# Attention through packed queries and a squared-ReLU layer on one core: the noughts' products between the first steps, 29 behind pv in place of 105 from the start

## The chip, the cores and the metric

The kernel runs on one core of a Trainium2 chip. The metric is device time in microseconds (us) from the launch to the end of the one program on that core; several runs are taken and their median is given. A core has a matrix engine (PE, with a weight loader written PEld in the profile), a vector engine (DVE), a scalar engine (ACT), a general engine (POOL), a queue engine (SP) that here only issues DMAs, and 16 DMA engines. Each engine works through its own list of instructions in order; where one needs another's result, it waits on a semaphore.

## What is computed

There are 8 batches of 8 heads, 576 rows per head and 64 columns, and 32 packed rows p per head. The reference is, cut to its core:

```python
def sm_attn(qq, kk, vv):
    s = scale * np.matmul(qq, kk.transpose(0, 1, 3, 2))
    s = s - np.max(s, axis=-1, keepdims=True)
    a = np.exp(s)
    a = a / (np.sum(a, axis=-1, keepdims=True) + 1e-09)
    return np.matmul(a, vv)
p_packed = sm_attn(p, k, v)              # 32 rows per head
out = sm_attn(q, p_packed, p_packed)     # 576 rows per head
x = out.transpose(0, 2, 1, 3).reshape(8 * 576, 8 * 64)
r = np.maximum(x @ w_in, 0.0)            # 4608 x 2048
result = (r * r) @ w_out                 # 4608 x 512, float32
```

The products on PE take bfloat16 operands and add up in float32.

## The kernel before, in words

Everything is written out by hand in one long string of words, `ORDER` (lines 50 to 142). `run` (line 778) takes it word by word, and each word puts the instructions of one small step at the end of the lists of the engines that it uses. So the string is the order on every engine, and nothing is rearranged later. A batch has two quads of four heads; the last two digits of a word such as `s100` are the batch and the quad. The words of batch 0, in the order in which they matter here:

- `pf`, `Lk`, `Lv`, `LA`, `LB`, `Wi`, `Wo` issue loads: the packed rows by SP, the keys, values, queries and weights by POOL. `P0` and `P1` scale the packed rows of two batches and turn them on DVE.
- `kT` turns the keys of one quad (DVE, line 361). `s1` multiplies them with the packed rows (PE, line 385: 24 products of 32 by 32 tiles per quad). `m1` takes the row maximum (DVE, line 411), `x1` the exponentials (ACT, line 423). `eT` turns them on PE (line 443), `eo` copies the turned block out of PSUM (DVE, line 431), and `rd` takes reciprocals of the sums.
- `pv` is the product with the values for both quads (PE, line 467). `pp` divides by the sums (DVE, line 480), `pt` turns that on PE (line 506) and `po` copies it out (ACT), and `bd` turns it in 32 by 32 blocks on DVE (line 488).
- `qA` and `qB` turn the first 256 and the last 320 queries (DVE, line 373). `zA` and `zB` multiply them with the packed result (PE, line 385 too). For each part then come the steps of the second softmax: `t` turn (DVE, line 528), `m` maximum (DVE, line 533), `s` difference (DVE, line 539, or POOL), `x` exponentials (ACT, line 545), `u` sums and reciprocals (DVE, lines 551 and 553), `a` product with these (POOL or DVE, line 559), `T` turn (DVE, line 573).
- `wa` and `wb` multiply the packed result into w_in (PE, line 584) and `Wa`, `Wb` copy it out. From there `h` is a block of the first layer (PE, line 600), `r` its ReLU, `q` the square into the tile gT, `o` a block of the second layer (PE, line 658), `c` a copy out of PSUM and `d` the store.

Batches overlap: while PE does `h` and `o` of one batch, the attention steps of the next stand between them. In batch 0 there is nothing to put between. There the string has words `Z` with a number, which call `busy` (line 341): so many products of a stretch of gT that holds noughts, as weights and as the moving operand, 288 columns wide, into a PSUM bank that nobody reads. No other engine waits for them, and they wait only once, for the memset of the noughts (line 197, DVE's first instruction). Being in PE's list like all else, the word that stands behind a `Z` starts no sooner than the `Z` has gone through. The order around them, lines 51 to 56 shortened to what stands on PE and what feeds it:

```python
Z32 s100 ... kT01 ... m100 Z4 s101 x100 m101 ... x101 Z13 eT00 eo00:v Z2 eT01 rd0 eo01:v
... Z4 pv0 pp0 qA01 Lk10 Z4 pt0 bd0 qA00 po0:a Z5 zA0 Lk11 tA00 tA01
mA01 mA00 sA01:v xA01 sA00:v uA01 xA00 qB00 Wo0 qB01 aA01:p uA00 Z33 zB0 wa00 Lv11
tB00 tB01 aA00:p Wa00:a mB00 Z5 wa01 mB01 sB00:p Wa01:a TA01 Z3 wb01 TA00 Lv10 wb00
```

The first `h` stands right behind these lines. The noughts' stretch of gT lies in a part that batch 3 fills much later.

Of the kernel before, what the change touches and what calls it, by code (L numbers as in the profile page):

```python
# [20 lines left out]
P = 128  # L21
# [3 lines left out]
S = T * NP  # L25
HALF = S // 2
# [24 lines left out]
pf Lk00 Lk01 Lv00 Lv01 I P0 LA0 P1 Wi00 kT00 Wi10 LB0 Z32 s100 Wi01  # L51
kT01 Wi11 m100 Z4 s101 x100 m101 Wi21 x101 Z13 eT00 eo00:v Z2 eT01 rd0 eo01:v
Wi20 Z4 pv0 pp0 qA01 Lk10 Z4 pt0 bd0 qA00 po0:a Z5 zA0 Lk11 tA00 tA01
mA01 mA00 sA01:v xA01 sA00:v uA01 xA00 qB00 Wo0 qB01 aA01:p uA00 Z33 zB0 wa00 Lv11
tB00 tB01 aA00:p Wa00:a mB00 Z5 wa01 mB01 sB00:p Wa01:a TA01 Z3 wb01 TA00 Lv10 wb00
xB00 sB01:v h0.0.8 h0.0.9 Wb01:a Wb00:v h0.0.1 h0.0.0 xB01 uB00 r0.0.8:a r0.0.1:a h0.0.2 uB01 r0.0.9:a aB00:p
r0.0.0:a h0.0.3 r0.0.2:v q0.0.4:a h0.0.11 Wo2 aB01:v h0.0.10 q0.0.0:a TB00 TB01 r0.0.3:a r0.0.10:v r0.0.11:a h0.1.0 h0.1.1
q0.0.1:v q0.0.5:a h0.1.9 r0.1.0:v h0.1.8 r0.1.1:a r0.1.9:v LA1 w100 w101 q0.1.0:v r0.1.8:a h0.1.10 W100:v W101:a h0.1.11
h0.1.3 q0.1.4:p h0.1.2 r0.1.10:a r0.1.3:v r0.1.11:a h0.0.4 kT10 r0.1.2:a LB1 h0.0.13 r0.0.4:a h0.0.5 q0.1.1:a h0.1.14 r0.0.13:v
q0.1.5:p h0.0.14 r0.0.5:v h0.1.13 r0.1.14:a kT11 h0.0.15 r0.0.14:a h0.0.6 q0.0.2:a h0.0.12 Wo1 r0.0.15:v s11 r0.1.13:a r0.0.12:v  # L60
r0.0.6:a Wo3 h0.1.15 q0.0.7:v q0.0.6:a h0.0.7 r0.1.15:v h0.1.4 r0.0.7:a Lv20 h0.1.6 m110 r0.1.4:a h0.1.5 r0.1.6:a h0.1.7
m111 h0.1.12 q0.0.3:a o2.0 x110 r0.1.5:v o2.1 r0.1.12:v q0.1.7:p o0.0 x111 o3.0 r0.1.7:a eT10 q0.1.6:a o0.1
Pr q0.1.2:v eT11 q0.1.3:v eo10:a o1.0 rd1 eo11:v o3.1 pv1 o1.1 pp1 o0.2 pt1 o1.2 bd1
po1:a o3.2 qA11 w011 w111 qA10 W011:a o0.3 W111:v o2.2 Lv21 o1.3 qB10 zA1 qB11 w010
o2.3 tA11 W010:a tA10 o3.3 mA11 zB1 mA10 sA11 w110 o0.4 sA10 tB11 W110:a o2.4 tB10
o1.4 mB11 xA11 o0.5 xA10 mB10 o1.5 uA10 o2.5 Lk20 sB11 o0.6 uA11 o0.7 xB11 aA10
o1.6 c0:a aA11 o1.7 sB10 o3.4 TA10 c1:a d0 TA11 o2.6 uB11 xB10 h1.0.1 Lk21 h1.0.6
Px o2.7 r1.0.1:v d1 r1.0.6:v o3.5 aB11 h1.0.0 c2:a h1.0.2 Pt o3.6 r1.0.0:a TB11 o3.7 r1.0.2:a
d2 Lk31 Pu:v q1.0.0:a h1.0.4 h1.0.3 c3:a o4.0 r1.0.3:v r1.0.4:a o5.0 kT20 q1.0.1:a h1.0.7 d3 h1.0.5
uB10 o5.1 r1.0.5:a o4.1 r1.0.7:v q1.0.2:a aB10 h1.0.10 h1.0.8 q1.0.3:v r1.0.10:a o4.2 kT21 Lq2 h1.0.9 r1.0.8:a  # L70
o5.2 r1.0.9:a h1.0.12 TB10 s12 q1.0.4:v r1.0.12:a h1.0.14 m120 o5.3 Lv30 r1.0.14:a h1.1.1 m121 h1.1.3 r1.1.1:a
o5.4 x120 r1.1.3:v h1.0.11 o4.3 r1.0.11:v x121 h1.1.7 kT31 h1.0.15 eT20 Lq3 q1.0.5:a o4.4 r1.0.15:v eT21
r1.1.7:v q1.0.7:a o5.5 rd2 eo20:v eo21:a h1.0.13 h1.1.2 r1.0.13:v o4.5 r1.1.2:v q1.0.6:a h1.1.6 pv2 r1.1.6:v h1.1.8
pp2 h1.1.0 q1.1.1:a r1.1.8:v Lk30 o5.6 qT21 q1.1.3:a o4.6 h1.1.12 r1.1.0:a bd2 pt2 qT20 o4.7 bs2:a
Lk40 h1.1.5 po2:v r1.1.12:a o5.7 q1.1.0:v c4:a h1.1.10 r1.1.5:v c5:a s22 d4 r1.1.10:v h1.1.4 o6.0 t221
r1.1.4:a h1.1.9 d5 o7.0 q1.1.2:a t220 h1.1.13 r1.1.9:a o6.1 qT30 r1.1.13:a Lq4 h1.1.11 q1.1.4:a m221 w120
w121 r1.1.11:a o6.2 m220 W121:a h1.1.14 h1.1.15 W120:v Lv31 o6.3 r1.1.14:a q1.1.6:a o7.1 o6.4 sb21:v r1.1.15:a
Lv40 o7.2 q1.1.5:a kT30 o7.3 q1.1.7:a o7.4 sb20:v Lk41 x221 o6.5 qT31 o7.5 x220 o6.6 su21
o6.7 o7.6 su20 c6:a o7.7 w020 a221 c7:a d6 w021 o8.0 W020:a a220 o8.1 d7 o8.2
aT21 W021:a o8.3 aT20 o8.4 Lq5 h2.0.1 h2.0.0 r2.0.1:v o8.5 r2.0.0:a o8.6 q2.0.0 h2.0.2 h2.0.3 r2.0.2:v  # L80
o9.0 Lk50 o8.7 r2.0.3:v h2.0.5 c8:a s13 q2.0.1 r2.0.5:a h2.0.4 d8 m130 o10.0 r2.0.4:a h2.0.6 kT40
h2.0.7 r2.0.6:a o10.1 r2.0.7:a q2.0.2 h2.0.10 Lk51 x130 m131 o9.1 h2.0.8 r2.0.10:a q2.0.3 o9.2 r2.0.8:a kT41
h2.0.13 x131 eT30 h2.0.9 r2.0.13:v o10.2 eo30:a rd3 r2.0.9:v h2.1.1 eT31 q2.0.4 h2.0.14 r2.1.1:a o10.3 r2.0.14:v
eo31:a h2.0.11 Lk61 o9.3 r2.0.11:v o9.4 h2.0.12 h2.1.5 q2.0.5 r2.0.12:a pv3 r2.1.5:v h2.0.15 q2.0.6 h2.1.4 pp3
r2.0.15:a o9.5 r2.1.4:v h2.1.6 bd3 pt3 q2.0.7 h2.1.0 bs3:a o9.6 r2.1.6:v r2.1.0:v Lv41 po3:a o9.7 q2.1.2
h2.1.8 q2.1.0 c9:a h2.1.2 r2.1.8:v s23 r2.1.2:a Lv50 d9 o11.0 t230 h2.1.3 h2.1.7 t231 o10.4 r2.1.3:a
w130 m230 r2.1.7:a w030 W130:a h2.1.10 q2.1.1 h2.1.9 q2.1.3 o10.5 W030:a m231 o10.6 o11.1 sb30:v r2.1.10:a
o11.2 r2.1.9:a sb31:v o10.7 x230 o11.3 q2.1.4 c10:a h2.1.15 qT40 o11.4 x231 h2.1.11 su30 r2.1.15:a w031
d10 r2.1.11:a w131 W031:a h2.1.14 su31 h2.1.13 o12.0 r2.1.14:a a230 o12.1 r2.1.13:a o12.2 W131:a q2.1.5 o12.3
a231 h2.1.12 o11.5 aT30 r2.1.12:a o12.4 aT31 o12.5 q2.1.6 q2.1.7 h3.0.5 h3.0.2 qT41 r3.0.5:a o12.6 h3.0.0  # L90
r3.0.2:v Lq6 o11.6 r3.0.0:a o12.7 h3.0.1 h3.1.1 r3.0.1:v c12:a o11.7 r3.1.1:v s14 d12 c11:a q3.0.0 h3.0.4
kT50 h3.0.3 r3.0.4:a o13.0 r3.0.3:a m140 d11 h3.0.9 Lk60 o14.0 r3.0.9:a q3.0.1 h3.1.3 x140 kT51 h3.1.0
o14.1 r3.1.3:a m141 o13.1 Lk70 r3.1.0:a h3.0.8 q3.0.2 eT40 x141 h3.0.7 r3.0.8:v o13.2 eo40:v r3.0.7:a h3.0.6
q3.1.0 o14.2 q3.0.4 r3.0.6:a eT41 rd4 q3.0.3 h3.0.11 eo41:a h3.1.2 r3.0.11:v o14.3 r3.1.2:v o13.3 h3.0.12 h3.0.10
q3.1.1 pv4 r3.0.10:a r3.0.12:v o14.4 Lv51 pp4 h3.0.13 q3.0.5 h3.0.14 r3.0.13:a bd4 o13.4 r3.0.14:v bs4:a pt4
Lv60 q3.0.6 h3.0.15 h3.1.8 o13.5 po4:v r3.1.8:a o14.5 r3.0.15:v s24 q3.0.7 h3.1.11 t240 h3.1.6 r3.1.11:a o13.6
t241 r3.1.6:a o13.7 w040 qT51 c13:a w041 h3.1.4 W040:a m241 o16.0 d13 h3.1.5 m240 r3.1.4:a o16.1
r3.1.5:a o14.6 W041:a sb41:v h3.1.9 h3.1.7 q3.1.2 o14.7 r3.1.7:a sb40:v r3.1.9:a w140 w141 x241 q3.1.3 h3.1.10
c14:v o16.2 W141:a h3.1.13 q3.1.4 d14 o15.0 su41 r3.1.10:a o16.3 x240 o15.1 r3.1.13:v W140:a h3.1.12 q3.1.5
o16.4 a241 o15.2 r3.1.12:a h3.1.14 su40 h3.1.15 o16.5 r3.1.14:a q3.1.6 o15.3 r3.1.15:a a240 o15.4 o16.6 q3.1.7  # L100
o15.5 aT40 aT41 o16.7 qT50 o15.6 c16:a h4.0.1 h4.0.4 Lq7 r4.0.1:v o15.7 d16 r4.0.4:v o17.0 c15:a
h4.0.3 h4.0.2 r4.0.3:v o17.1 r4.0.2:a d15 s15 q4.0.1 h4.0.0 kT60 h4.0.9 o17.2 r4.0.0:a m151 o17.3 r4.0.9:a
h4.0.6 m150 o17.4 r4.0.6:a h4.1.3 q4.0.0 x151 o17.5 kT61 o18.0 x150 o17.6 r4.1.3:v Lk71 h4.0.5 h4.0.13
rd5 r4.0.5:a o18.1 r4.0.13:v eT50 h4.0.11 eo50:v h4.0.12 eT51 q4.0.2 o17.7 r4.0.12:v r4.0.11:a o18.2 eo51:a c17:v
h4.1.2 h4.0.10 q4.0.6 r4.1.2:a pv5 d17 r4.0.10:a h4.0.7 Lv61 q4.1.1 h4.0.15 r4.0.7:a o19.0 q4.0.5 r4.0.15:a pp5
o19.1 q4.0.3 o19.2 Lv71 bd5 h4.0.8 pt5 bs5:v h4.1.11 r4.0.8:a o18.3 po5:v q4.0.4 h4.1.1 s25 r4.1.11:a
r4.1.1:v o18.4 qT60 h4.1.0 o18.5 t251 h4.1.6 o19.3 r4.1.0:a t250 r4.1.6:a o18.6 q4.1.0 h4.0.14 h4.1.10 m251
r4.0.14:a w050 r4.1.10:a w150 q4.0.7 W050:a h4.1.4 m250 h4.1.7 o18.7 r4.1.4:v W150:a o19.4 r4.1.7:v o19.5 q4.1.5
c18:a o19.6 q4.1.3 sb50:v o19.7 d18 h4.1.8 qT61 c19:a o20.0 x250 h4.1.5 sb51:v o21.0 d19 r4.1.5:a
o20.1 r4.1.8:a su50 o21.1 x251 h4.1.12 q4.1.2 h4.1.9 r4.1.12:a w151 a250 r4.1.9:a w051 h4.1.15 W151:a su51  # L110
o20.2 o21.2 r4.1.15:a q4.1.4 o21.3 W051:a a251 o20.3 h4.1.14 aT50 h4.1.13 aT51 s16 r4.1.14:a r4.1.13:v o20.4
kT70 h5.0.6 h5.0.8 r5.0.6:a m160 o20.5 r5.0.8:a h5.0.0 q4.1.7 o21.4 x160 m161 h5.0.4 o21.5 r5.0.0:a q4.1.6
eT60 r5.0.4:a kT71 h5.0.9 h5.0.1 x161 o20.6 r5.0.9:v o20.7 eo60:v r5.0.1:a h5.0.5 rd6 q5.0.4 c20:a eT61
r5.0.5:v h5.0.7 o21.6 q5.0.0 eo61:a q5.0.2 h5.0.10 d20 o22.0 r5.0.7:v r5.0.10:a o21.7 q5.0.3 h5.0.3 h5.0.2 c21:v
r5.0.3:a pv6 r5.0.2:a h5.1.0 d21 pp6 Lv70 h5.0.11 q5.0.1 r5.1.0:a o23.0 bd6 pt6 r5.0.11:v h5.0.13 bs6:a
# [29 lines left out]
class Kernel:  # L145
# [195 lines left out]
    def busy(self, n):  # L341

        ps = self.banks("idle").tile([P, 512], F32, name="ps_idle")
        for _ in range(n):
            self.nc.tensor.matmul(ps[:, :HALF], lhsT=self.nought[:, :P], rhs=self.nought, start=True, stop=True)  # L345
# [402 lines left out]
    def step(self, word):  # L748
        word, _, e = word.partition(":")
        engine = self.engines.get(e, self.nc.vector)  # L750
        q4 = self.NFB // 4
# [81 lines left out]
```

## Time and profile before

| what | value |
|---|---|
| three runs | 243.76, 243.35, 243.53 us; median 243.53 us |
| span of the profiled execution | 241.6 us (first to last instruction of the program) |
| PE busy | 235.7 us, 98% of the span, 2461 products |
| DVE, ACT, POOL busy | 203.3 us (84%), 142.0 us (59%), 74.7 us (31%) |
| products of noughts | 105, from 1.1 to 20.8 us |

The profile gives the profiled execution its span alone, and no other time of its own. The median of the runs is 1.9 us above that span; these 1.9 us lie before the program's first instruction and behind its last. Every position below is counted from the span's start. A product of PE is shown from its issue to its modelled end, so products that follow each other overlap in the rows; the distance from start to start is what each costs in a stream. In the views, "idle before <-X" is the time in which the engine had nothing to do just before that instruction and what ended it.

### The profile page before, as it was taken

To read this page: it belongs to the slowest core of one execution; us is meant where nothing else is said; L and a number is where in the kernel's file an instruction comes from. 1 tells how busy PE (TensorE), PEld (TensorE's weight loads), DVE (VectorE), ACT (ScalarE), POOL (GpSimd) and SP (SyncE) were. 2 spreads that over 40 slices of the span, in tenths; PEclk is the share of its full clock that TensorE was granted. 3 is DMA by queue.
4 is the path that set the end of the run, shared out by engine and by line. 5 is a ranking of instruction groups with operands and counts; after the bars stand their busy time and mean duration, and the time that the engine had idled before them with its cause. 6 is when DMAs were issued, how large, how long until landed. Compare 5 with 4: busy or idle time off the path is not lost.

```text
span 241.6 us, 6190 instructions
## 1 busy us (share of the span) xinstructions
PE 235.7 (98%) x2461; PEld 130.8 (54%) x2461; DVE 203.3 (84%) x459; ACT 142.0 (59%) x308; POOL 74.7 (31%) x123
## 2 busy tenths in 40 slices
PE   8999899999999999999999999999999999999994
PEld 5775564456544565456554654465545645565543
DVE  2679986999998789989998889997899879987650
ACT  2216993697898567956693647774495346733300
POOL 8636784594586163044403340002000000000000
PEclk9999999999999999999999999999999999999999
DMA  6999999999999979249932984317113211211224
GB/s 104 192 200 210 203 207 206 173 180 219 200 189 188 252 104 127 60 60 220 104 90 29 204 114 53 71 26 113 27 26 81 49 43 43 46 43 43 46 63 110
DMA packets 33404, 28.51 MB, mean 118 GB/s; under 512 B 8160, under 2 KB 28384, under 8 KB 33376
## 3 DMA queue, kind: packets, MB, share of 16 engines
q0 software_dynamic: 26848, 18.55, 54.4%
q1 hardware_dynamic: 6384, 9.51, 14.9%
q8 instruction: 19, 0.31, 0.5%
q14 instruction: 9, 0.07, 0.1%
q10 hardware_dynamic: 144, 0.07, 0.1%
HBM read 37.22 MB, written 9.44 MB: 193 GB/s over the span
## 4 chain that ended last, share of the span: by engine, by line
PE 94%; ACT 2%; DMA 2%; DVE 1%; SPq 0%; issue 0%; ACTq 0%; DVEq 0%
PE ps_o L658 52%; PE ps_h L600 26%; PE ps_idle L345 4%; PE ps_wp L584 4%; PE ps_s L385 3%; PE ps_e1T L443 2%; DMA gT<-in_p_dram 2%; PE ps_pv L467 1%; ACT r L605 1%; ACT gT L643 0%; PE ps_ppT L506 0%; ACT wp L429 0%; PE ps_o L663 0%; DVE kT L361 0%; SPq L278 0%; ACT e L545 0%
## 5 line engine op out<-in xcount | busy, mean ns | idle before, releaser
L658 PE MATMUL ps_o<-w_out_bf,gT 128*128 128x512 bf16 (+1 forms) x576 | 147.3, 378 | 0.0
L600 PE MATMUL ps_h<-a2T,wp 128*128 128x288 bf16 (+2 forms) x512 | 89.9, 286 | 1.3 <-DVE rs L553 0.6
L605 ACT ACTIVATE r<-ps_h 128x288 bf16<-128x288 f32 (+2 forms) x159 | 61.0, 415 | 47.2 <-PE ps_h L600 43.9
L658 PEld LDWEIGHTS <-gT 128*128 128x128 bf16 x576 | 54.4, 98 | 43.1 <-issue 3.2
L600 PEld LDWEIGHTS <-wp 128*128 128x128 bf16 x512 | 47.7, 98 | 42.4 <-issue 8.0
L607 DVE TENSOR_SCALAR r<-ps_h 128x288 bf16<-128x288 f32 (+2 forms) x97 | 41.8, 446 | 11.2 <-PE ps_h L600 10.6
L645 DVE TENSOR_TENSOR gT<-r 128x576 bf16<-128x576 bf16 (+2 forms) x104 | 45.1, 445 | 2.8 <-ACT r L605 1.8
L429 ACT CAST wp<-ps_wp 128x1024 bf16<-128x1024 f32 (+1 forms) x29 | 27.7, 974 | 9.1 <-PE ps_wp L584 9.0
L429 ACT COPY o_sb<-ps_o 128x512 f32<-128x512 f32 x26 | 15.2, 589 | 12.3 <-PE ps_o L658 11.9
L278 POOL DMA_DIRECT2D k_b<-in_k_dram x28 | 15.2, 544 | 16.2 <-DVE kT L361 7.6
L278 POOL DMA_DIRECT2D q_b<-in_q_dram x16 | 10.9, 684 | 29.9 <-DVE qT L373 25.4
L323 POOL DMA_DIRECT2D v_b<-in_v_dram x12 | 9.4, 781 | 31.5 <-PE ps_pv L467 30.5
L345 PE MATMUL ps_idle<-gT 128*128 128x288 bf16 x105 | 16.7, 314 | 1.1 <-DVE gT L197 1.1
L423 ACT ACTIVATE e<-ps_s,nm 128x576 bf16<-128x576 f32 x16 | 11.8, 742 | 7.6 <-DVE nm L411 7.6
L643 ACT ACTIVATE gT<-r 128x512 bf16<-128x512 bf16 (+1 forms) x21 | 14.0, 689 | 0.5 <-DVE r L607 0.3
L545 ACT ACTIVATE e<-d 128x576 f32<-128x576 f32 (+2 forms) x20 | 11.6, 599 | 4.2 <-DVE d L539 3.9
L345 PEld LDWEIGHTS <-gT 128*128 128x128 bf16 x105 | 10.6, 107 | 5.1 <-DVE gT L197 1.1
L411 DVE TENSOR_REDUCE nm<-ps_s 128x1 f32<-128x576 f32 x16 | 11.5, 740 | 1.2 <-PE ps_s L385 1.2
L373 DVE STREAM_TRANSPOSE qT<-q_b 128x576 uint32<-128x576 uint32 (+2 forms) x20 | 12.4, 631 | 0.0
L361 DVE STREAM_TRANSPOSE kT<-k_b 128x576 uint32<-128x576 uint32 x16 | 12.3, 767 | 0.1
L551 DVE TENSOR_REDUCE sums<-e 128x18 f32<-128x576 f32 (+2 forms) x20 | 12.2, 608 | 0.1
L533 DVE TENSOR_REDUCE mx<-s 128x18 f32<-128x576 f32 (+2 forms) x20 | 11.6, 609 | 0.0
(60 smaller groups left out, 185.3 us busy)
## 6 DMA issues: line engine op xcount, KB each, us to landing
out_dram<-o_sb SPq DMA_DIRECT2D x65, 128.0 KB, 3.0
v_b<-in_v_dram POOLq DMA_DIRECT2D x12, 256.0 KB, 6.4
w_out_bf<-in_moe_w_out_dram POOLq DMA_DIRECT2D x4, 512.0 KB, 12.2
q_b<-in_q_dram POOLq DMA_DIRECT2D x6, 288.0 KB, 5.6
q_b<-in_q_dram POOLq DMA_DIRECT2D x12, 144.0 KB, 6.3
k_b<-in_k_dram POOLq DMA_DIRECT2D x12, 108.0 KB, 3.6
gT<-in_v_dram POOLq DMA_DIRECT2D x4, 288.0 KB, 9.5
w_in_bf<-in_moe_w_in_dram POOLq DMA_DIRECT2D x4, 256.0 KB, 10.2
```

The lines of the kernel that those rows point to most:

```text
L278: engine.dma_start(x[n:], s[:P - n])
L345: self.nc.tensor.matmul(ps[:, :HALF], lhsT=self.nought[:, :P], rhs=self.nought, start=True, stop=True)
L361: self.nc.vector.transpose(t["kT"][:].rearrange("p s e -> p (s e)").bitcast(U32), t["k"][:].rearrange("p t d -> p (t d)").bitcast(U32))
L373: self.nc.vector.transpose(out.bitcast(U32), x.bitcast(U32))
L429: engine.copy(out, x)
L551: nc.vector.reduce_sum(out=sums[:, x], in_=t["e2"][:, x], axis=AX.X)
L600: self.nc.tensor.matmul(ps, lhsT=t["wp"][:, fb // n, fb % n * P:(fb % n + 1) * P], rhs=t["a2T"][:, s0:s1], start=(qd == 0), stop=(qd == se ...
L605: engine.activation(r, ps, ACT.Relu)
L607: engine.tensor_scalar_max(r, ps, 0.0)
L643: engine.activation(out, r, ACT.Square)
L645: engine.tensor_tensor(out=out, in0=r, in1=r, op=ALU.mult)
L658: self.nc.tensor.matmul(self.o[tt][:, e], lhsT=self.gT[:, fb, a:a + P], rhs=self.w_out_bf[:, fb, e], start=(i == 0), stop=(i == self.NFB - 1))
```

## The change

A word `Z` now carries two numbers, so many products of 512 columns and so many of 256, and the stretch of noughts grows from 288 to 512 columns, so that its memset does too. The five words ahead of `pv0` (`Z32`, `Z4`, `Z13`, `Z2`, `Z4`: 55 products) are gone. The five behind it stay at their places: `Z4` becomes `Z2.0`, `Z5` becomes `Z2.1` (twice), `Z33` becomes `Z18.1`, `Z3` becomes `Z1.1`. That is 25 products of 512 and 4 of 256 columns, 13,824 columns, the sum of 27 full ones, where 50 products of 288 had 14,400 columns; ahead of `pv0` 15,840 columns are gone. The string is broken into lines differently, so the lines of the program below it move up by ten. Every other word stands where it stood, and the lists of DVE, ACT, POOL and SP are the same.

```diff
-pf Lk00 Lk01 Lv00 Lv01 I P0 LA0 P1 Wi00 kT00 Wi10 LB0 Z32 s100 Wi01
-kT01 Wi11 m100 Z4 s101 x100 m101 Wi21 x101 Z13 eT00 eo00:v Z2 eT01 rd0 eo01:v
-Wi20 Z4 pv0 pp0 qA01 Lk10 Z4 pt0 bd0 qA00 po0:a Z5 zA0 Lk11 tA00 tA01
-mA01 mA00 sA01:v xA01 sA00:v uA01 xA00 qB00 Wo0 qB01 aA01:p uA00 Z33 zB0 wa00 Lv11
-tB00 tB01 aA00:p Wa00:a mB00 Z5 wa01 mB01 sB00:p Wa01:a TA01 Z3 wb01 TA00 Lv10 wb00
+pf Lk00 Lk01 Lv00 Lv01 I P0 LA0 P1 Wi00 kT00 Wi10 LB0 s100 Wi01 kT01 Wi11 m100 s101 x100 m101 Wi21 x101 eT00 eo00:v eT01
+rd0 eo01:v Wi20 pv0 pp0 qA01 Lk10 Z2.0 pt0 bd0 qA00 po0:a Z2.1 zA0 Lk11 tA00 tA01 mA01 mA00 sA01:v xA01 sA00:v uA01 xA00
+qB00 Wo0 qB01 aA01:p uA00 Z18.1 zB0 wa00 Lv11 tB00 tB01 aA00:p Wa00:a mB00 Z2.1 wa01 mB01 sB00:p Wa01:a TA01 Z1.1 wb01
...
-        self.nought = self.gT[:, 0, 3 * S:3 * S + HALF]
+        self.nought = self.gT[:, 0, 3 * S:3 * S + self.NE]
...
-    def busy(self, n):
+    def busy(self, n, short):
 
         ps = self.banks("idle").tile([P, 512], F32, name="ps_idle")
-        for _ in range(n):
-            self.nc.tensor.matmul(ps[:, :HALF], lhsT=self.nought[:, :P], rhs=self.nought, start=True, stop=True)
+        for m in [self.NE] * n + [self.NE // 2] * short:
+            self.nc.tensor.matmul(ps[:, :m], lhsT=self.nought[:, :P], rhs=self.nought[:, :m], start=True, stop=True)
...
-            self.busy(int(word[1:]))
+            self.busy(*map(int, word[1:].split(".")))
```

## The prediction

> **What bounds the kernel now.** I read the page's busy times first, then PE's timeline of the first 28 us, then busy times by stage, and last the noughts' own rows. The page says that PE is the bound, and that the noughts lie on the chain that ended last:
>
> ```profile
> PE 235.7 (98%) x2461; PEld 130.8 (54%) x2461; DVE 203.3 (84%) x459; ACT 142.0 (59%) x308; POOL 74.7 (31%) x123
> ...
> L345 PE MATMUL ps_idle<-gT 128*128 128x288 bf16 x105 | 16.7, 314 | 1.1 <-DVE gT L197 1.1
> ```
>
> The same by stage (window, its length, then each engine's busy time, the clock, the DMA share):
>
> ```profile
> 7.50:15.00 7.50, 7.48 (x160) 5.34 (x160) 4.68 (x11) 2.04 (x5) 3.52 (x6) 1.00 1.33 199
> 15.00:19.50 4.50, 4.50 (x57) 3.20 (x55) 4.03 (x13) 0.75 (x2) 2.65 (x5) 1.00 1.37 203
> 19.50:28.40 8.90, 7.62 (x89) 4.22 (x82) 8.74 (x23) 7.87 (x19) 5.52 (x8) 1.00 1.19 205
> 28.40:238.40 210.00, 209.93 (x2134) 113.90 (x2133) 183.22 (x406) 129.78 (x281) 56.62 (x92) 1.00 0.65 110
> ```
>
> From 28.4 us on PE is idle for 0.07 of 210 us: whatever time the steps before it lose or win, the end loses or wins. From 19.5 to 28.4 us DVE (third number) is busy for 8.74 of 8.90 us, so DVE sets that stretch, and the moment that counts is when it begins: DVE's first turn behind `zB0`, at 19.48 us. Before that PE looks full, but mostly with noughts; its timeline (start, length, and what it did):
>
> ```profile
> 1.08 6.21 PE L345 MATMUL ps_idle<-gT 128*128 128x288 bf16 x32 [1.08 <-DVE gT L197]
> 7.52 0.69 PE L385 MATMUL ps_s<-kT,pT 32*32 32x192 bf16 x24 [0.23 <-DVE kT L361]
> 8.15 0.66 PE L345 MATMUL ps_idle<-gT 128*128 128x288 bf16 x4
> 8.74 0.69 PE L385 MATMUL ps_s<-kT,pT 32*32 32x192 bf16 x24
> 9.36 1.77 PE L345 MATMUL ps_idle<-gT 128*128 128x288 bf16 x13
> ...
> 12.47 0.58 PE L467 MATMUL ps_pv<-gT,e1T 96*32 96x64 bf16 x48
> 12.98 0.66 PE L345 MATMUL ps_idle<-gT 128*128 128x288 bf16 x4
> ...
> 14.43 0.42 PE L385 MATMUL ps_s<-qT,ppd 32*32 32x256 bf16 x16
> 14.78 4.22 PE L345 MATMUL ps_idle<-gT 128*128 128x288 bf16 x33
> 18.93 0.47 PE L385 MATMUL ps_s<-qT,ppd 32*32 32x320 bf16 x16
> ```
>
> 32 products took 6.21 us at the start, 33 took 4.22 us later. The noughts' rows up to 5 us and behind 5.7 us (shortest, median, longest of one in ns) say why:
>
> ```profile
> L345 PE MATMUL ps_idle<-gT x17: 423/447/448, 1.1 to 4.9; 128*128 128x288 bf16 x17
> L345 PE MATMUL ps_idle<-gT x13: 286/286/286, 5.5 to 7.0; 128*128 128x288 bf16 x13
> ```
>
> From start to start one costs (4.22 - 0.29) / 32 = 0.123 us late, and in the first four us, by the trace's starts, 0.240 us: PE begins at half speed. The switch comes at 5.44 us, 4.36 us after its first product. (The page's clock row reads 9 throughout; it shows no early half clock, the durations do.) So before `s100`, the first useful product, PE has been brought to full speed by products that delay nothing: `s100` waited 0.23 us for DVE.
>
> **What the change does, part by part.** What PE sends during its first 4 us of dense work runs at half speed. The change moves that stretch from idle time onto the steps of batch 0.
>
> *Removed, ahead of pv.* 55 products. `Z32` frees nothing, `s100` waits for `kT` at 7.47 us. The others delayed their successors: `s101` had its keys at 8.31 and began at 8.74 us; `eT01` could start at about 11.15, when `x101` was read out, and began at 11.55 us.
>
> *The price of half speed on useful steps.* The trace has no small product at half clock. From the noughts, a step grows by 447/286 = 1.56 if its last product's length rules and by 0.240/0.123 = 1.95 if its stream rules. These steps are short, so I take 1.65 and keep both ends (about 0.2 us at `zB0` apart). Through the chain, with the other engines' lengths and hand-overs (about 0.05 us) as they are:
>
> - `s101` begins at 8.48, when the slower `s100` has streamed (8.74 before), lasts 1.14 (0.69) to 9.62 (9.43).
> - `m101`, `x101` follow: `m101` at 9.67 (9.48), `x101` read out at 11.29 (11.11).
> - `eT01` from 11.35 (11.55), 0.82 long (0.50), to 12.17 (12.05); its copy `eo01` to 12.77 (12.64).
> - second half of `pv` ends at 13.33 (13.05), so `pp` starts at 13.40 (13.13) and ends at 13.83.
>
> Up to here 0.27 us late: what the noughts' absence gives nearly pays for the clock.
>
> *Changed, behind pv.* In columns every word is smaller than before (1,024 for 1,152; 1,280 for 1,440; 9,472 for 9,504), but they cost by time. A 512-wide product at full clock is in the second layer's rows: 20 of them in 4.32 us, 0.216 us each. At half clock I estimate 512/288 x 0.240 = 0.427 us.
>
> - `Z2.0` behind `pv`: 2 x 0.427 = 0.85 where four took 0.49; it ends at about 14.0, behind `pp`'s end: `pt0` at 14.0 (13.61).
> - `Z2.1`: 2.5 x 0.427 = 1.07 (0.61). `zA0` is ready at 14.65 but starts at 15.3 (14.43), ends at 15.95 (14.85). Late by 1.0 to 1.1 us; DVE's eleven instructions up to `qB01` follow, to 19.75 (18.73).
> - `Z18.1` starts at 15.7 (14.78) and lasts 18 x 0.216 + 0.109 = 4.0 us at full clock, and half of what is left of the half-clock time more. I count the dense work from `pv`'s first half at about 11.95: plus 4.36 us gives full clock at 16.3, so 0.6 us of `Z18.1` is slow and it ends at 15.7 + 4.0 + 0.3 = 20.0. `zB0` then starts at 20.0 (18.93), DVE behind it at 20.5 (19.48).
> - `Z2.1` and `Z1.1` behind that are at full clock and a little shorter (0.54 for 0.61, 0.32 for 0.37); the words behind them wait for buffers that DVE and ACT free: nothing gained.
>
> *Unchanged or nearly.* The wider memset (0.18 us now, at most 0.1 more) lies in DVE's idle 1.33 us before its first use of the packed rows. No DMA moves past another; POOL's issues that wait for DVE come later with it, and the weights have time (`o2.0` at 33.3 us). No wait is added: PE has nothing queued for the noughts but their memset, done long before.
>
> **Sum:** DVE's turn at 20.5 instead of 19.48, +1.0 us. Span 241.6 + 1.0 = 242.6; the runs' median lies 1.9 above the span, which the change leaves: 243.53 + 1.0 = **244.5 us**.
>
> The unknown is which work brings up the clock. Recomputing the chain for other moments of full clock: 11 us gives -0.4, 12 gives -0.2, 13.5 gives 0, 14.5 +0.2, 15 +0.5, 16.3 +1.0, 17.5 +1.6, 18.5 +2.1, 19.6 +2.6. (Behind 15.7 us each us later costs half a us: a slow product does half its work.)
>
> A rule bears on this. The Trainium skill, "TensorE: Matmul & The Clock Gate", Part 1, says that the array stays at half rate until one busy window of about 3.4 us has passed, and that the windows run freely, whenever the kernel starts. The trace's 4.36 us agree with it. Counted from `pv`'s second half at 12.8 us, full clock would come between 16.2 and 19.6 us by that page, and the sum would be +1.0 to +2.6 us. The same section calls the warming's cost under 1% of a usual span, which either end of that is near.
>
> **The rivals.**
>
> - *The small products bring up the clock.* `s100` to `eT01` keep PE busy for 3.7 us between 7.5 and 12.2 us, with one gap of 0.8 us. For it: the trace shows no threshold. Against: they are a few tiles of 32, 25% of the array, or turns, with gaps, while the noughts that raised it filled all of it without one. If full clock comes at 11 us, `eT01` and all behind it run at full speed, the removed noughts' delay is won back: `pp` 0.25 us earlier, `zA0` at 14.15, `Z18.1` ends at 18.5, -0.4 us: 243.1. It ends not slower if full clock comes before 13.5 us; up to 14.9 us it costs under 0.5.
> - *The clock comes up late.* Noughts behind `pv` stand between short steps; if only an unbroken stretch counts, it begins with `Z18.1` at 15.3 to 15.7 us, and full clock comes at 18.5 to 20 us: +2.1 to +2.8, 246.0. Against: between `pv` and `Z18.1` PE does not pause.
> - *The change is not felt:* PE starts at full clock when nothing ran before. The 447 ns rows say otherwise. The noughts' delay alone is won, -0.5 us or a little more: 243.0.
>
> **How the numbers follow.** About 0.2% (0.49 us) is what a measurement of this kernel can tell from no change. The forecast (full clock from 15 to 17.5 us): 0.42, all slower. Late clock: 0.18, slower. Small products (before 15 us): 0.35, of it 0.31 same and 0.04 faster. Not felt: 0.05, half faster, half same. So slower 0.60, same 0.33, faster 0.07. The range takes in -0.4 of the early clock and +2.4 of the late one: 243.1 to 245.9; outside are the later half of the late case (0.09) and about 0.06 below.
>
> **What would show it.** Right: rows of `s` at line 385 of over 1 us each near 7.5 and 8.5 us; `zA0` near 15.3; the first of the 512-wide noughts 0.43 us apart and later ones 0.216; the 18 ending near 20 us, with DVE's turn 0.5 us behind; the same 8.9 us from there to full PE. Wrong: `eT01` already in 0.50 us (clock up early), or DVE's stretch behind `zB0` shorter than before, so that the delay is not passed on.

## The result, and the profile after

Six runs of the changed kernel took 244.49 to 245.40 us, median **245.16 us**; six runs of the kernel before, 243.35 to 243.76, median 243.50. The ratio is 1.0058, with a 95% interval of 1.0046 to 1.0070: slower by 1.66 us in the medians. The profiled execution took 245.24 us with a span of 243.4, 1.8 us longer than the span before.

The stages of the changed kernel, moved to where its own stages lie (window, length, busy time of PE, PEld, DVE, ACT, POOL, then clock, DMA share, GB/s), with the line of PE's busy time from the page ahead of them:

```profile
PE 230.5 (95%) x2385; PEld 124.7 (51%) x2385; DVE 203.6 (84%) x459; ACT 142.0 (58%) x308; POOL 74.7 (31%) x123
```

```profile
21.00:30.20 9.20, 7.82 (x102) 4.09 (x87) 8.79 (x23) 7.89 (x19) 5.24 (x8) 1.00 1.21 207
30.20:240.20 210.00, 209.93 (x2134) 113.87 (x2133) 183.44 (x406) 129.78 (x281) 56.61 (x92) 1.00 0.64 109
```

PE's busy time fell by 5.2 us and the span grew by 1.8: busy time is no measure here. The last 210 us are the same, the 9 us of DVE's stretch too, both 1.8 us later (the window is 9.20 us long because it begins 0.25 us ahead of DVE's turn; from that turn to PE's block behind it are 8.90 us, 8.89 before). So the loss arose before 21 us. PE's timeline there:

```profile
7.20 2.19 PE L375 MATMUL ps_s<-kT,pT 32*32 32x192 bf16 x48 [7.20 <-DVE kT L351]
...
13.08 1.03 PE L335 MATMUL ps_idle<-gT 128*128 128x512 bf16 x2
13.91 0.42 PE L496 MATMUL ps_ppT<-ident,pp 128*128 128x128 bf16 x2
14.17 1.22 PE L335 MATMUL ps_idle<-gT 128*128 128x512 bf16 x3
15.33 0.62 PE L375 MATMUL ps_s<-qT,ppd 32*32 32x256 bf16 x16
15.88 4.89 PE L335 MATMUL ps_idle<-gT 128*128 128x512 bf16 x19
20.70 0.47 PE L375 MATMUL ps_s<-qT,ppd 32*32 32x320 bf16 x16
```

The 19 noughts' products in place of 33 narrow ones (4.22 us) took 4.89, and `zB0` stands behind them. The first softmax part's scores (15.33) took 0.62 us where they took 0.42. Then DVE's first turn behind `zB0`, before and after, with its idle time in brackets:

```profile
19.48 0.52 DVE L528 STREAM_TRANSPOSE s<-ps_s 128x320 f32<-128x320 f32 x1 [0.22 <-PE ps_s L385]
21.25 0.52 DVE L518 STREAM_TRANSPOSE s<-ps_s 128x320 f32<-128x320 f32 x1 [0.88 <-PE ps_s L375]
```

DVE waited 0.88 us for PE there, 0.22 before; the turn is 1.77 us later, and that is nearly the whole change of the span. One product of the first scores (shortest, median, longest in ns) shows the half clock, before and after:

```profile
L385 PE MATMUL ps_s<-kT,pT x48: 240/242/258, 7.5 to 9.2; 32*32 32x192 bf16 x48
L375 PE MATMUL ps_s<-kT,pT x48: 314/357/360, 7.2 to 9.0; 32*32 32x192 bf16 x48
```

The noughts' own rows say when the clock rose:

```profile
L335 PE MATMUL ps_idle<-gT x4: 507/620/634, 15.9 to 17.1; 128*128 128x512 bf16 x4
L335 PE MATMUL ps_idle<-gT x17: 272/379/634, 16.7 to 20.5; 128*128 128x512 bf16 x16, 128*128 128x256 bf16 x1
```

In the trace's starts they are 0.427 us apart at first and 0.216 us from 17.4 us on, where the clock's record begins. (The clock column says 1.00 before a record begins, whatever the clock is: 1.00 from 7.50 to 15.00 us here.) So PE ran at half clock from the first scores at 7.20 to 17.38 us.

### The profile page after: what moved, and what is told of

The parts are those of the page before. It is cut to its first block, busy times and chain, and to the rows that moved or that the text cites. A ratio compares the mean times of both kernels' runs of the same rounds, so it can differ in the third digit from the quotient of the medians.

```text
span 243.4 us, 6038 instructions
## 1 busy us (share of the span) xinstructions
PE 230.5 (95%) x2385; PEld 124.7 (51%) x2385; DVE 203.6 (84%) x459; ACT 142.0 (58%) x308; POOL 74.7 (31%) x123
## 4 chain that ended last, share of the span: by engine, by line
PE 93%; ACT 2%; DMA 2%; DVE 1%; SPq 0%; issue 0%; ACTq 0%; DVEq 0%
PE ps_o L648 51%; PE ps_h L590 26%; PE ps_wp L574 4%; PE ps_s L375 4%; PE ps_idle L335 3%; PE ps_e1T L433 2%; DMA gT<-in_p_dram 2%; PE ps_pv L457 1%; ACT r L595 1%; ACT wp L419 1%; ACT gT L633 0%; PE ps_ppT L496 0%; PE ps_o L653 0%; ACT e L413 0%; DVE nm L401 0%
## 5 line engine op out<-in xcount | busy, mean ns | idle before, releaser
L648 PEld LDWEIGHTS <-gT 128*128 128x128 bf16 x576 | 54.4, 98 | 43.1 <-issue 3.2
L375 PE MATMUL ps_s<-kT,pT 32*32 32x288 bf16 (+1 forms) x288 | 5.8, 294 | 7.2 <-DVE kT L351 7.2
L529 DVE TENSOR_TENSOR d<-s,mx 128x576 f32<-128x576 f32 (+2 forms) x19 | 11.6, 630 | 0.0
```

Of the source, the lines that this page charges most:

```text
L375: self.nc.tensor.matmul(ps[c, hf, :s1 - s0], lhsT=x[hf % len(x)][r].rearrange("p (i e) -> p i e", e=2)[:, :, e], rhs=y[r, s0:s1, e], start ...
L648: self.nc.tensor.matmul(self.o[tt][:, e], lhsT=self.gT[:, fb, a:a + P], rhs=self.w_out_bf[:, fb, e], start=(i == 0), stop=(i == self.NFB - 1))
```

## The experiments

All were timed beside the kernel before on the same chip, whose median was 243.44 us in the first four and 243.45 in the second four. Behind each median stand the lowest and the highest run, and behind each ratio to the kernel before its 95% interval.

**The first word alone, put back.** (`e1_front`) One word more in the changed kernel:

```diff
-... kT00 Wi10 LB0 s100 ...
+... kT00 Wi10 LB0 Z18.0 s100 ...
```

> The changed kernel with one word more: 18 products of 512 columns (as many columns as the old first word) ahead of the first scores; nothing between the scores and pv. Theory (the loss is half clock on the steps and on the noughts themselves): full clock before 7.5 us; the steps up to pv run at full speed and are no longer held by noughts, so DVE's first turn behind zB0 comes 0.5 to 1.0 us before 19.48: 242.5 to 243.1 us, faster than both kernels, unless the gaps before pv drop the clock again. Rival A (wide noughts behind pv cost by their width or shape, not by the clock): stays near 245.1. Rival B (the pauses before pv drop the clock within a window): full clock is lost between 9 and 13 us, 244 to 245.5.

Measured 243.78 us (242.78 to 244.37), 1.0008 of the kernel before (0.9996 to 1.0020): nearly all of the loss is gone, and no gain is there. The time lies between the theory's 242.5 to 243.1 and rival B's 244 to 245.5. Wide noughts behind `pv` are not the cost. The stages of its profile are cut here at the clock's record:

```profile
4.30:7.60 3.30, 2.85 (x32) 1.38 (x33) 1.41 (x4) 0.00 (x0) 3.30 (x6) 1.00 1.11 185
7.70:11.00 3.30, 1.83 (x46) 1.23 (x36) 2.42 (x5) 1.67 (x4) 1.58 (x3) 1.00 1.27 195
11.10:14.40 3.30, 2.88 (x54) 1.37 (x55) 1.78 (x5) 0.37 (x1) 1.44 (x3) 0.50 1.39 200
14.50:17.90 3.40, 3.40 (x32) 1.54 (x32) 2.75 (x9) 0.75 (x2) 1.13 (x3) 1.00 1.38 198
```

Full, full, half, full, in steps of 3.41 us: by its mechanism rival B, which is also the theory's own condition. PE was busy for 1.83 of 3.30 us behind the scores, and the clock fell for the next step, though no pause was longer than this one:

```profile
9.66 0.54 PE L433 MATMUL ps_e1T<-ident,e 128*96 128x128 bf16 x6 [0.82 <-ACT e L413]
```

The other runs have no trace, but each has its mean granted clock, and one step at half clock brings that to 0.993 (half of 3.41 us out of 241.8). Nine of the twelve runs have 0.990 to 0.993 and took 243.44 to 244.37 us; the three with 1.000 took 242.78, 243.03 and 243.45. By this record the clock does not fall in every run, and the runs in which it falls are longer by some 0.8 us (medians 243.79 and 243.03).

**The narrow products, only behind pv.** (`e2_narrow`) The kernel before without `Z32`, `Z4`, `Z13`, `Z2`, `Z4`:

> The kernel before without its five words of noughts ahead of pv; behind pv the 50 products of 288 columns as before. Theory: the width does not matter, the clock does: rows of the steps ahead of pv as in the changed kernel, full clock in the same stretch of time (16 to 19 us), 245.0 to 245.6 us. Rival A (the loss comes from the 512-wide products behind pv): 243.1 to 243.6.

Measured 245.73 us (244.73 to 245.86), ratio 1.0085 (1.0069 to 1.0101). That is 0.13 us above the range. Its profile, of the fastest of the six runs (244.73 us), has full clock from 15.85 us. 50 narrow products cost as much as 29 wide ones or more: the width is not the cause.

**No noughts at all.** (`e3_none`) The changed kernel without its five `Z` words:

> The changed kernel without any products of noughts. Theory: the steps up to zB0 run at half clock but wait for nothing, so zB0 starts near 19.1 us and DVE's turn near 19.8 (0.3 behind the kernel before); then the first layer's blocks run at half clock until 3.4 to 7 us after about 21.5 us, which makes PE the bound there: 0.3 + 0.9 to 2.1, so 244.7 to 245.9 us. Rival A (the wide noughts are the cost): 243.2 to 243.8, better than the changed kernel by over 1 us. Rival C (the first layer's slow start costs more than the noughts): above 246.

Measured 244.44 us (244.18 to 245.03), ratio 1.0043 (1.0030 to 1.0056): below the range by little, and 0.7 us *better* than the changed kernel. DVE's turn came at 19.89 us, 1.36 before that of the changed kernel, and the first layer then ran at half clock up to 24.76 us (the kernel before did the same products in 272 ns by the median; its row stands first):

```profile
L600 PE MATMUL ps_h<-a2T,wp x10: 269/272/273, 21.6 to 23.3; 128*128 128x256 bf16 x10
L590 PE MATMUL ps_h<-a2T,wp x12: 334/421/421, 22.3 to 24.6; 128*128 128x256 bf16 x12
```

So noughts that first have to bring up the clock themselves, with steps queued behind them, cost more than they saved here.

**The kernel before without its first word.** (`e4_no_first`) Only `Z32` is taken out:

> The kernel before without its first word alone (32 products before the first scores); the four other words ahead of pv stay, so PE is busy without a pause from about 7.3 us on. Theory, if every product counts for the clock: full clock 3.4 to 4.4 us after the scores begin, near 11 to 12 us, eT00 near 12.8 us, all later steps 1.8 us late: 245.3 us. Rival D (products on few tiles do not count, only full-array ones): full clock no sooner than 3.4 us behind the 13 noughts' start at 10.4 us, 14 us or later; eT00 near 13.5 us, and 2.5 to 3.5 us late: 246 to 247.

Measured 245.62 us (244.47 to 246.22), ratio 1.0083 (1.0062 to 1.0104), and full clock at 12.91 us. The time speaks for the theory; the moment lies between the two. The step of the clock that ended at 9.49 us was streamed for only 0.53 of its length and had not been enough. (Streamed means the share of the time in which columns go through PE; the last section says how it was worked out.)

**Do products on few tiles count?** (`e6_tiles`) The changed kernel with 160 products of the scores' form ahead of the scores (a new word `Y40`; each of its 40 rounds is this, one product for each of four heads):

```diff
+            for h in range(QH):
+                x = slice(NP * h, NP * h + NP)
+                self.nc.tensor.matmul(ps[x, :S // 3], lhsT=self.nought[x, :NP], rhs=self.nought[x, :S // 3], start=True, stop=True)
```

> The changed kernel with 160 small products of noughts ahead of the first scores, in the scores' own form (32 by 32 tiles, 192 columns, four at a time), and no full-array product before pv. If any streaming counts for the clock: full clock between 4.5 and 8 us, the first scores' row 0.69 us long, then as e1_front: 243.0 to 244.4 us. Rival D (few tiles do not count): groups 0.16 us apart up to 7.6 us, the scores' rows 1.15 us each, full clock only from 14 us on: 245.0 to 245.8 us.

```profile
1.19 4.92 PE L343 MATMUL ps_idle<-gT 32*32 32x192 bf16 x160 [1.19 <-DVE gT L187]
7.25 0.69 PE L383 MATMUL ps_s<-kT,pT 32*32 32x192 bf16 x24 [1.15 <-DVE kT L359]
```

The scores take 0.69 us, full clock, and its record begins at 4.20 us: rival D falls: products on a quarter of the array raise the clock too. (The step before was streamed for 0.88 of its length, so a somewhat smaller weight of such products is not excluded.) The time, 243.99 us (242.86 to 245.54; ratio 1.0010, 0.9991 to 1.0028), spreads by 2.7 us; in the profiled execution, the slowest, the clock fell at 11.03 us and rose only at 17.86. Six of its ten runs have a granted clock of 0.985 to 0.993 and took 243.78 to 245.54 us; of the four with 0.997 or more, three took 242.86 to 243.10 and one 244.82. So the median, inside the expected 243.0 to 244.4, lies between runs of both kinds.

**Fewer noughts behind pv.** (`e7_short`) `Z1.0`, `Z1.1`, `Z13.1` for `Z2.0`, `Z2.1`, `Z18.1`:

> The changed kernel with fewer noughts behind pv: one of 512 ahead of pt0, one and a half ahead of zA0, 13 and a half ahead of zB0. Theory (the noughts' own length at half clock holds zA0 and zB0): zA0 near 14.8 and DVE's turn near 20.1 us where the changed kernel had 15.3 and 21.25: 243.8 to 244.5 us. Rival A' (only the useful steps at half clock cost): no better than 245.0. Rival C (fewer noughts leave the clock at half when the first layer begins): 244.5 to 245.2, with slow rows at line 590.

Measured 244.78 us (244.01 to 245.06), ratio 1.0047 (1.0031 to 1.0063): a miss by 0.3 us. `zA0` did come sooner, but the step of the clock that ended at 15.68 us was streamed for only about 0.7 of its length, and the clock rose at 19.09 us, so that 14 products took as long as 19 had:

```profile
15.47 4.86 PE L335 MATMUL ps_idle<-gT 128*128 128x512 bf16 x14
20.26 0.47 PE L375 MATMUL ps_s<-qT,ppd 32*32 32x320 bf16 x16
```

**Noughts ahead of the scores, none later.** (`e8_front_only`) `Z18.0` in front of `s100`, all five others out:

> The changed kernel with 18 wide products ahead of the first scores and no others. Theory: scores at full clock, half clock from between 9 and 13 us on, DVE's turn near 19.4 us, and the first layer's first blocks at half clock as in e3_none: 243.5 to 244.3 us, 0.4 to 0.8 below e3_none. Rival (the clock outlasts the pauses): 242.5 to 243.0.

Measured 243.80 us (243.39 to 245.25), ratio 1.0013 (0.9999 to 1.0026), inside the theory's range. The clock falls when PE thins out, and returns with the first layer's dense work:

```profile
9.50:12.80 3.30, 1.72 (x60) 1.25 (x60) 1.95 (x6) 1.17 (x4) 1.56 (x3) 1.00 1.35 198
12.90:16.20 3.30, 0.93 (x18) 0.42 (x19) 2.52 (x9) 0.37 (x1) 1.25 (x3) 0.50 1.32 203
...
23.10:26.50 3.40, 3.40 (x17) 2.08 (x15) 2.82 (x9) 3.26 (x9) 2.14 (x3) 0.50 1.13 206
```

**Noughts that fit the waits.** (`e5_fitted`) The changed kernel with four words more ahead of `pv`:

```diff
-LB0 s100 ... m100 s101 ... x101 eT00 eo00:v eT01
+LB0 Z18.0 s100 ... m100 Z1.0 s101 ... x101 Z3.1 eT00 eo00:v Z1.1 eT01
```

> The changed kernel with 18 wide products ahead of the first scores, and between the steps up to pv only so many as fit the waits that the run e1_front shows at full clock (1 of 512 ahead of s101; 3 and a half ahead of eT00; one and a half ahead of eT01). Theory (the clock's windows of 3.41 us are judged by how much of them PE streams: 37% let it fall in e1_front, 79% raised it): every window after the first rise is filled by over 50%, the clock stays full, and DVE's turn behind zB0 comes 11.2 us after the first scores where the kernel before took 12.0: 242.6 to 243.0 us, faster than the kernel before. Rival A (the pauses' idle time, not the clock, sets these steps): 243.4 to 243.8 as e1_front. Rival B (the window still counts as idle): clock at half between 9 and 15 us, 243.8 or more.

Measured **242.93 us** (242.52 to 243.32), ratio 0.9978 (0.9968 to 0.9988): better than both kernels. The clock is full from 3.85 us to the end of the span, and no run of the twelve has a mean granted clock under 0.998: none lost a step. PE's list up to the second `eT`, with the pauses filled:

```profile
7.09 0.69 PE L375 MATMUL ps_s<-kT,pT 32*32 32x192 bf16 x24 [0.54 <-DVE kT L351]
7.71 0.39 PE L335 MATMUL ps_idle<-gT 128*128 128x512 bf16 x1
8.18 0.69 PE L375 MATMUL ps_s<-kT,pT 32*32 32x192 bf16 x24
8.81 0.93 PE L335 MATMUL ps_idle<-gT 128*128 128x512 bf16 x3
9.69 0.54 PE L433 MATMUL ps_e1T<-ident,e 128*96 128x128 bf16 x6
10.06 0.49 PE L335 MATMUL ps_idle<-gT 128*128 128x512 bf16 x2
10.60 0.54 PE L433 MATMUL ps_e1T<-ident,e 128*96 128x128 bf16 x6
```

DVE's turn behind `zB0` comes 11.40 us after the first scores (expected 11.2; 11.96 before), and without idle time, so PE no longer holds DVE there:

```profile
18.49 0.91 DVE L518 STREAM_TRANSPOSE s<-ps_s 128x320 f32<-128x320 f32 x2
```

## Why the prediction was right, and where it was off

The first scores began between 7.09 and 7.56 us in the ten profiles, a spread that does not go with the edits (7.09 us in e3_none and in e5_fitted, 7.55 and 7.56 in e7_short and e8_front_only: without and with noughts ahead of them); so positions are compared from there (7.52 before, 7.20 after).

- *The mechanism and the place* held: half clock on the steps, then on the noughts themselves, and DVE's turn behind `zB0` as the point that is passed on in full. 1.77 us there, 1.8 in the span. Counted from the first scores the turn came 14.05 us after them, 11.96 before: 2.09 us late, of which this execution got 0.32 back because its scores began earlier.
- *Half clock on useful steps.* Predicted, `pp` 5.88 us after the first scores; measured 5.99 (before 5.61). The first scores took 1.15 us, predicted 1.14. The factor 1.65 was good. `pp` was 0.38 us late where 0.27 was predicted, so the noughts' absence paid for most of the clock's cost up to there.
- *The noughts behind pv.* 0.427 and 0.216 us each, as estimated. `zA0` came 8.12 us after the first scores, predicted 7.8, and `Z18.1` 8.7 us after them, predicted 8.2. DVE's first turn behind `zA0` was by then 1.42 us later than before (8.83 and 7.41 us after the scores). Up to `qB01` DVE has ten instructions there, not eleven; their time was read rightly.
- *The mis-sized term: full clock at 16.3 us.* It came at 17.38, 10.2 us after the first scores and not 8.8. `zB0` came 13.5 us after them, predicted 12.5. Half of this 1.0 us is the later start of `Z18.1`, behind steps and noughts at half clock that took a little longer than the working gave them. The other half is its length, 4.8 us from start to start for 4.3, and that is the clock. The working let the 4.36 us of the dense start run from `pv`'s first half. The runs show that it is no length that runs from a start: the clock is set anew at fixed steps of 3.41 us (every stretch between two changes of the recorded clock is a whole number of them: 6.83 and 3.41 us in e1_front, 6.83 and 13.65 in e8_front_only), by how full the step just gone was. The step from 10.56 to 13.97 us, with `eT` and `pv` and their gaps, was streamed for 0.69 and not full enough; the next one, with 0.91, was.
- *How much of it was luck.* 10.2 us after the first scores are 17.7 us in the prediction's own positions, just behind the 15 to 17.5 us that it forecast, and its list gives about +1.7 there. The medians gave +1.66. The two agree closely by luck in part: the turn was 2.09 us late, and the earlier start of the scores took 0.32 of that back. The direction came from the mechanism; that the time stayed in the range came from a range that also took in the late clock.
- *The rival of the early clock* had its counter-argument half wrong. Small tiles do count (e6_tiles). What kept the clock down were the gaps: the steps 7.14 to 10.56 and 10.56 to 13.97 us were both streamed for 0.69 of their length. That it would not come true was right, for one of the two reasons given.
- *The rival of the late clock* is the same mechanism where a step falls short: 19.09 us in the profile of e7_short, which has fewer noughts and its steps at other positions. Where the steps lie relative to the kernel's start differs from run to run, which fits the spread of 0.9 us in the changed kernel's six runs against 0.4 before. That it sets each run's time was not shown for this kernel: only one execution has a trace, and the granted clock of the others (0.998 to 1.000) leaves out the half clock ahead of its first record. In e1_front the two went together.
- *Not felt* is excluded: the steps behind 7.20 us ran at half clock.

## What to carry to other kernels

Products of noughts pay where PE would be idle anyway and nothing is queued behind them; the same products put between waiting steps must be sized by the time that they take at the clock that PE has then, not by columns. Bring up the clock in the time that the first loads leave free, and then keep the pauses between small steps filled to just below each wait. And read a PE that is busy for less while the kernel gets longer as a sign that what is left runs slower: compare durations of one form, not busy shares.

## What was not expected of the hardware

The share of a step that PE streams was worked out for the ten profiles from the traces' starts, columns and clock, with 512 columns as 0.427 us at half clock and half of that at full; records that a trace lacks were put in. Steps of 3.41 us that were streamed for up to 0.77 left the half clock as it was (0.77 in e6_tiles, one lacking record put in), and such from 0.78 on raised it: 0.78 in e3_none and e5_fitted, 0.81 in e2_narrow, 1.00 before. This working does not tell 0.77 from 0.78 surely, so the border is known as near 0.77 and no closer. The full clock fell behind steps of 0.30, 0.31 and 0.37 (e6_tiles, e8_front_only, e1_front) and stayed behind one of 0.48 (the changed kernel, 24.2 to 27.6 us); no run shows what lies between. So in these runs it took a fuller step to raise the clock than to keep it.

The Trainium skill, "TensorE: Matmul & The Clock Gate", Part 1, has the 3.4 us window and its free run, and both agree with the records (steps of 3.41 us, at another place in each profile). The same page of the Trainium skill, "Why this matters for your kernels", advises against idle gaps over some 3 us. In e1_front the clock fell with no gap over 0.82 us in the step before; the gaps there added up to a step that was streamed for 0.37.
